# K and V in eight-partition groups: each group takes 1 MB that lies in one go in HBM

## The chip, the cores and the metric

The kernel runs on one core of a Trainium2 chip. The metric is the device time of one launch in microseconds, the median of several runs. A core has engines that work side by side and meet only through semaphores: PE (TensorE, matrix multiply, with its weight loads shown as PEld), DVE (VectorE), ACT (ScalarE), POOL (GpSimd) and SP (SyncE, which here only issues DMAs). Sixteen DMA engines move data between HBM, the large memory, and SBUF, the working memory of 128 partitions. One DMA that is issued on SP is shared out among them.

## The reference

One token is decoded. With g = sigmoid(sum of x times gate_w), the result is g times an attention block plus (1 - g) times a gated feed-forward block. The attention has 32 heads of 128, each over 65536 cached keys and values:

```python
q = (x @ wq).reshape(B, Sq, H, Dh).transpose(0, 2, 1, 3)        # one query per head
scores = jnp.einsum("bhqd,bhkd->bhqk", q, k_cache) * (Dh ** -0.5)
p = softmax(scores, axis=-1)
o = jnp.einsum("bhqk,bhkd->bhqd", p, v_cache)
a = o.transpose(0, 2, 1, 3).reshape(B, Sq, H * Dh) @ wo
b = (silu(x @ w_gate) * (x @ w_up)) @ w_down
return g * a + (1 - g) * b
```

All inputs are bf16. k_cache and v_cache have the shape [1, 32, 65536, 128]; a head of either is 16.78 MB. x has 512 elements, and the weights together are 14.0 MB.

## The kernel before

K and V pass through SBUF once. A head's 65536 rows are seen as 128 partitions times R = 512 rows. They are loaded in two halves, z = 0 and z = 1, of HR = 256 rows per partition each, so one load is 8.39 MB, with 64 KB for each partition. The view that a load reads is `kv_dram` (L200). In it the halves are the slowest dimension, then the partitions, then a partition's 256 rows: half z is one stretch of 8.39 MB in HBM, and partition p has the p-th 64 KB of it.

All loads go to one tile, `mem`, 184 KB per partition, in places that share it in turn: K half 0 at KA, K half 1 at KZ, V half 0 at VA and V half 1 at VZ. They overlap, so a load waits until the engines have read what it overwrites.

SP's program (L212 to L250) sets the order of the loads. The weights come first (L203 to L205). The first half of K of head 0 is issued as two loads of half the size (L219 to L222), with 32 KB for each partition, so that the work can begin on the first. Then come, for each head h from 1 on (L224 to L236): K half 0 of head h, V half 0 of head h - 1, K half 1 of head h, V half 1 of head h - 1. Before each stands a wait for DVE (`ktdone`) or PE (`pvdone`), which tells that the place is free. At the end come wo and the V of the last head, in eight pieces of falling size (`tail`, L59, issued at L239 to L245).

For K, DVE transposes blocks of 32 rows (L403 for half 0, L410 for half 1, L334 for head 0) into `kt`, and PE multiplies them with the head's query into the scores psS (L460): each partition and row gives one score, in one column of psS. ACT takes the exponential (L305), DVE shuffles its result into pb (L343), and PE multiplies pb with V into psO (L507), row by row of the places VA and VZ. For the last head, `piece` (L521) does the same with the pieces of the tail. A score of column r in partition p is multiplied by the row of V that lies in the same partition p and at the same row r; neither the largest score nor the sums ask which key that was.

## Time and profile before

| What | Value |
|---|---|
| Median of 3 runs | 2519.66 us (2519.46 to 2519.95) |
| The profiled execution's own time | 2521.24 us |
| Its span, from the first to the last instruction | 2519.9 us |
| Granted TensorE clock, mean | 0.71 |
| Busy: PE, PEld, DVE, ACT, POOL | 63%, 35%, 55%, 3%, 1% |
| Read from HBM | 1087.77 MB |

The page cuts the span into 40 slices of 63 us. For each it gives the busy share of the engines in tenths, the busy share of the core's 16 DMA engines, and the GB/s that they moved. Busy times of different engines lie beside each other and can't be added. A line of waits names who waited, for whom, the total in microseconds, how often, and the longest. A line of DMA issues gives a load's source, how many there were and the median time from issue to landing; it includes the time behind other loads in the queue.

### The profile page before, as it was taken

What the parts mean: (1) busy time and instruction counts of PE and PEld (TensorE: products, weight loads), DVE (VectorE), ACT (ScalarE), POOL (GpSimd) and SP (SyncE); (2) the same over time, 40 slices, a digit from 0 to 9 for tenths busy, and PEclk for the clock granted to TensorE, in tenths of its full rate; (3) what the DMA queues carried; (4) which work ended last, traced back from release to release, by engine and by line L of the source; (5) the groups of instructions that cost most, each with busy time, mean ns of one, the idle gap of its engine ahead of it and who ended that gap; (6) DMA issues with size and microseconds to landing.
All of it is one profiled execution on the core that took longest, in us unless ns stands there. A gap on an engine that the chain in (4) does not pass through costs nothing.

```text
span 2519.9 us, 46367 instructions
## 1 busy us (share of the span) xinstructions
PE 1586.7 (63%) x21432; PEld 890.3 (35%) x21432; DVE 1398.3 (55%) x1631; ACT 65.6 (3%) x195; POOL 26.8 (1%) x83
## 2 busy tenths in 40 slices
PE   3556756666666576565675665766656656567667
PEld 3333333333333333333333333333333333333334
DVE  3764565554654645646446555466464564654653
ACT  0000000000000000000000000000000000000000
POOL 0000000000000000000000000000000000000000
PEclk8567767677676676676776767767767667677676
DMA  9999999999999999999999999999999999999999
GB/s 420 434 433 433 433 434 433 433 433 433 434 434 433 433 432 435 433 434 435 433 433 436 434 435 433 433 434 433 433 435 433 434 432 433 433 433 434 432 433 387
DMA packets 20476, 1088.00 MB, mean 432 GB/s; under 512 B 2282, under 2 KB 2668, under 8 KB 2924
## 3 DMA queue, kind: packets, MB, share of 16 engines
q1 hardware_dynamic: 20452, 1087.78, 99.9%
q8 instruction: 11, 0.18, 0.0%
q14 instruction: 5, 0.04, 0.0%
q10 hardware_dynamic: 8, 0.00, 0.0%
HBM read 1087.77 MB, written 0.00 MB: 432 GB/s over the span
## 4 chain that ended last, share of the span: by engine, by line
DMA 73%; DVE 14%; issue 11%; PE 1%; DVEq 0%; SPq 0%; ACT 0%
DMA mem<-in_A_k_cache_dram 71%; DVE kt L410 7%; DVE kt L403 6%; DMA mem<-in_A_wo_dram 1%; PE psO L507 1%; DMA mem<-in_A_v_cache_dram 1%; DVE kt L334 0%; DVE pb L343 0%; DVEq L408 0%; SPq L205 0%; DVEq L401 0%; PE psS L460 0%; PE psZ L560 0%; SPq L220 0%; ACT fin L312 0%
## 5 line engine op out<-in xcount | busy, mean ns | idle before, releaser
L460 PE MATMUL psS<-qcur,kt 128*128 128x4 bf16 x16384 | 516.7, 167 | 886.1 <-DVE kt L403 552.0
L507 PE MATMUL psO<-mem,pb 128*4 128x512 bf16 x3968 | 1001.1, 418 | 17.4 <-DMA mem<-in_A_v_cache_dram 17.4
L403 DVE STREAM_TRANSPOSE kt<-mem 128x2048 uint32<-128x2048 uint32 x248 | 551.2, 2280 | 578.9 <-DMA mem<-in_A_k_cache_dram 577.9
L460 PEld LDWEIGHTS psS<-qcur,kt 128*128 128x128 bf16 x16384 | 474.0, 104 | 954.9 <-DVE kt L403 585.2
L410 DVE STREAM_TRANSPOSE kt<-mem 128x2048 uint32<-128x2048 uint32 x248 | 547.5, 2274 | 407.7 <-DMA mem<-in_A_k_cache_dram 407.7
L507 PEld LDWEIGHTS psO<-mem,pb 128*4 128x4 bf16 x3968 | 355.3, 91 | 619.8 <-issue 188.5
L343 DVE COPY pb<-pa 32x64 bf16<-32x64 bf16 x1024 | 234.1, 229 | 25.5 <-PE psO L507 10.7
L334 DVE STREAM_TRANSPOSE kt<-mem 128x2048 uint32<-128x2048 uint32 x16 | 35.4, 2275 | 17.0 <-DMA mem<-in_A_k_cache_dram 17.0
L348 DVE TENSOR_REDUCE sm<-psS 128x1 f32<-128x512 f32 x32 | 22.1, 691 | 35.5 <-PE psS L460 35.5
L299 ACT ACTIVATE oTn<-psT,gcol 128x1 bf16<-128x1 f32 x31 | 8.2, 263 | 1111.8 <-PE psT L487 1111.8
L278 POOL PARTITION_ALL_REDUCE sm<-sm x32 | 11.2, 351 | 2392.0 <-DVE sm L348 2392.0
L487 PEld LDWEIGHTS psT<-unit,orow 4*128 4x128 f32 x256 | 30.8, 186 | 14.9 <-issue 13.5
L487 PE MATMUL psT<-unit,orow 4*128 4x1 f32 x256 | 33.5, 248 | 0.8 <-ACT orow L297 0.8
L297 ACT ACTIVATE orow<-psO,sm 4x512 f32<-4x512 f32 x31 | 21.0, 677 | 447.7 <-issue 447.7
L303 ACT ACTIVATE sm<-sm 128x1 f32<-128x1 f32 x32 | 6.5, 203 | 831.7 <-POOL sm L278 831.7
L305 ACT ACTIVATE pa<-psS,sm 128x512 bf16<-128x512 f32 x32 | 22.0, 687 | 1.0
L521 PE MATMUL psW<-pb,mem 128*128 128x1 bf16 x512 | 14.4, 165 | 6.9 <-DMA mem<-in_A_v_cache_dram 5.7
L521 PEld LDWEIGHTS psW<-pb,mem 128*128 128x128 bf16 x512 | 13.9, 102 | 8.1 <-issue 6.4
L280 POOL PARTITION_ALL_REDUCE sm<-sm x32 | 12.3, 383 | 36.4 <-ACT pa L305 36.4
L444 PE MATMUL psM<-xTb,mem 128*128 128x1 bf16 x128 | 3.6, 166 | 11.6 <-DMA mem<-in_A_wq_dram 11.6
L536 PE MATMUL psY<-mem,oR 128*1 128x512 bf16 x31 | 9.6, 485 | 0.3 <-DVE oR L424 0.3
L430 DVE TENSOR_SCALAR w<-psW,sm 128x2 bf16<-128x2 f32 x1 | 0.2, 224 | 16.9 <-PE psW L521 16.9
(64 smaller groups left out, 62.0 us busy)
## 6 DMA issues: line engine op xcount, KB each, us to landing
mem<-in_A_v_cache_dram SPq DMA_DIRECT2D x3, 4096.0 KB, 28.9
mem<-in_A_k_cache_dram SPq DMA_DIRECT2D x2, 4096.0 KB, 38.7
mem<-in_A_wq_dram SPq DMA_DIRECT2D x1, 4096.0 KB, 13.1
mem<-in_A_wo_dram SPq DMA_DIRECT2D x1, 3968.0 KB, 34.3
mem<-in_A_v_cache_dram SPq DMA_DIRECT2D x1, 2048.0 KB, 33.4
mem<-in_B_w_gate_dram SPq DMA_DIRECT2D x1, 1792.0 KB, 16.9
mem<-in_B_w_up_dram SPq DMA_DIRECT2D x1, 1792.0 KB, 21.2
mem<-in_B_w_down_dram SPq DMA_DIRECT2D x1, 1792.0 KB, 25.0
```

The lines of the kernel that those rows point to most:

```text
L280: nc.gpsimd.partition_all_reduce(Lt, rsum, P, RADD).then_inc(s_L, 1)
L297: nc.scalar.mul(orow[0:4, :], psO[0:4, :], Li[0:4, :]).then_inc(s_or, 1)
L305: nc.scalar.activation(pa[:], psS[:], ACT.Exp, bias=nbias, scale=SCALE, accum_out=rsum).then_inc(expdone, 1)
L334: nc.vector.transpose(kt[:, i % 2, :].rearrange("p (j r t) -> p r j t", j=2, t=32), src.rearrange("p (r j t) -> p r j t", j=2, t=32)).then ...
L343: last = nc.vector.tensor_copy(dst, sr)
L348: nc.vector.reduce_max(mxs, psS[:], AX_X).then_inc(s_mx, 1)
L403: nc.vector.transpose(kt[:, c % 2, :].rearrange("p (j r t) -> p r j t", j=2, t=32), src.rearrange("p (r j t) -> p r j t", j=2, t=32)).then ...
L410: nc.vector.transpose(kt[:, c % 2, :].rearrange("p (j r t) -> p r j t", j=2, t=32), src.rearrange("p (r j t) -> p r j t", j=2, t=32)).then ...
L460: last = nc.tensor.matmul(psS[:, col + 4 * r:col + 4 * r + 4], ktb[c % 2][:, je // 2, r, :, je % 2], qcur[:, je, :], start=(je == 0), stop ...
L487: last = nc.tensor.matmul(psT[:, 0:1], orow[0:4, i * Dh:(i + 1) * Dh], unit[0:4, i:i + 1], start=(i == 0), stop=(i == 3))
L507: last = nc.tensor.matmul(psO[0:4, :], pb[:, 256 * z + r:256 * z + r + 4], vt[:, r * Dh:(r + 4) * Dh], start=(z == 0 and part == 0 and m = ...
L521: last = nc.tensor.matmul(psW[:, 0:1], vt[:, r * Dh:(r + 1) * Dh], pb[:, col:col + 1], start=(col == 0), stop=(col == R - 1))
```

## The change

The view of a head's rows in HBM changes. Before, the dimensions were, slowest first, half (b, 2), partition (p, 128), row (r, 256). After, they are group (e, 16), half (b, 2), partition within the group (k, 8), row (r, 256). Partition p is now 8e + k. Eight partitions together hold one stretch of 1 MB, of which half 0 is the first 512 KB and half 1 the second. One load is then 16 stretches of 512 KB, one every 1 MB. The destination is the same [128, n] slice of `mem` as before. The view has one dimension more, so the column slices of the first K load and of the tail get one more colon. The tail uses the same view. `lanes` is a new function around the destination that returns its argument.

```diff
         def kv_dram(cache, h):
-            return cache[0, h].rearrange("(b p r) d -> b p (r d)", b=2, p=P)
+            return cache[0, h].rearrange("(e b k r) d -> b e k (r d)", b=2, k=8, e=16)
+
+        def lanes(ap):
+            return ap
...
-                sp.dma_start(at(place(kind, h, z), HR * Dh), kv_dram(cache, h)[z]).then_inc(d[kind + "az"[z]], 16)
+                sp.dma_start(lanes(at(place(kind, h, z), HR * Dh)), kv_dram(cache, h)[z]).then_inc(d[kind + "az"[z]], 16)
...
-                sp.dma_start(at(KA + 32 * n, half), kv_dram(A_k_cache, 0)[0][:, n * half:n * half + half]).then_inc(
+                sp.dma_start(lanes(at(KA + 32 * n, half)),
+                             kv_dram(A_k_cache, 0)[0][:, :, n * half:n * half + half]).then_inc(
                     (d["ka0"], d["ka"])[n], 16)
...
-            src = A_v_cache[0, H - 1].rearrange("(b p r) d -> b p (r d)", b=2, p=P)
+            src = kv_dram(A_v_cache, H - 1)
...
-                sp.dma_start(at(kb, nr * Dh), src[b][:, o * Dh:(o + nr) * Dh]).then_inc(dt_[n], 16)
+                sp.dma_start(lanes(at(kb, nr * Dh)), src[b][:, :, o * Dh:(o + nr) * Dh]).then_inc(dt_[n], 16)
```

## The prediction

> **What bounds the kernel now.** I read the page first, its parts 1 to 3, to see which resource is full; then the stretches of the span, to see whether it is full in every stage; then the DMA queue's issues and waits, to see whether it ever runs dry; then the chain.

> ```profile
> span 2519.9 us, 46367 instructions
> PE 1586.7 (63%) x21432; PEld 890.3 (35%) x21432; DVE 1398.3 (55%) x1631; ACT 65.6 (3%) x195; POOL 26.8 (1%) x83
> DMA  9999999999999999999999999999999999999999
> GB/s 420 434 433 433 433 434 433 433 433 433 434 434 433 433 432 435 433 434 435 433 433 436 434 435 433 433 434 433 433 435 433 434 432 433 433 433 434 432 433 387
> DMA packets 20476, 1088.00 MB, mean 432 GB/s; under 512 B 2282, under 2 KB 2668, under 8 KB 2924
> q1 hardware_dynamic: 20452, 1087.78, 99.9%
> ```

> No engine that computes is over 63% busy. SP's queue keeps the 16 DMA engines busy for 99.9% of the span, and the rate is the same line of 432 to 436 GB/s in every slice but the first and the last. That is 433 / 16 = 27.1 GB/s for each DMA engine. A rate so level, whatever else is going on, is that of a fixed path, not of a memory that is busier at one time than at another.

> ```profile
> 200.00:600.00 400.00, 253.77 (x3379) 140.81 (x3376) 228.32 (x256) 10.07 (x30) 3.67 (x10) 0.70 1.00 434
> 1000.00:1077.40 77.40, 49.91 (x653) 27.47 (x652) 43.46 (x50) 2.02 (x6) 0.73 (x2) 0.71 1.00 434
> 2000.00:2400.00 400.00, 258.58 (x3311) 140.95 (x3312) 218.20 (x252) 11.14 (x34) 4.40 (x12) 0.71 1.00 434
> ```

> The columns are window, length, busy time of PE, PEld, DVE, ACT and POOL, granted TensorE clock, DMA share and GB/s. The second row is one head: in 77.4 us the DMA never rests, PE works 49.9 us and DVE 43.5 us.

> ```profile
> mem<-in_A_k_cache_dram SPq DMA_DIRECT2D x63, 29.7
> mem<-in_A_v_cache_dram SPq DMA_DIRECT2D x62, 26.1
> SPq L216 <- PE psO L507: 1314.4, 61, 25.0
> DVE kt L403 <- DMA mem<-in_A_k_cache_dram: 577.9, 30, 19.6
> DVE kt L410 <- DMA mem<-in_A_k_cache_dram: 407.7, 31, 13.7
> DMA 73%; DVE 14%; issue 11%; PE 1%; DVEq 0%; SPq 0%; ACT 0%
> ```

> A load of half a head is 32768 x 128 x 2 B = 8.39 MB, 19.4 us at 433 GB/s. From issue to landing a K load takes 29.7 us and a V load 26.1 us, so a load waits 10.3 or 6.7 us behind the one before it: the queue has no gaps, although SP waits for free buffers. DVE waits for K 985.6 us in all. The chain's 11% "issue" and 14% DVE are steps of that same wait for K, beside DMA that goes on working.

> **The sum that the change acts on.** K and V are 32 x 2 x 16.78 MB = 1073.7 MB of the 1087.8 MB, 98.7%. Of the 99.9% x 2519.9 = 2517.4 us of DMA, 2484.9 us are K and V. The profiled execution took 2521.2 us, 1.3 us more than its span and 1.6 us over the median of 2519.66; the sum is made against 2521.2, and 1.6 is taken off at the end.

> **The change part by part.**

> *The issue on SP.* The source gets one more dimension (16 groups of 8 runs in place of 128 runs). L216 shows an issue at 328 ns; there are 125 of those, and 2 + 8 others for K and V. The trace has no issue with such a source; the others on SP take 400 to 530 ns (the weights' issues, L205). I bound it between 0 and +0.33 us each, 0 to 41 us on SP for the 125. The cover is the 6.7 us that each load is issued ahead of its turn, so I take 0; without the cover it would be those 41 us. Behind an issue in SP's program stands the next wait for a buffer, which lasts up to 25.0 us, and nobody waits for SP itself.

> *The runs.* A partition's share of a load is 256 rows, 64 KB in one piece in HBM, before and after; the first K load's two halves have 32 KB each. The 128 runs of a load, and the 20476 packets, should stay. Cost 0, the cover being none: if runs were cut smaller it would be seen in the packet count.

> *Which rows lie where.* Column r of partition p now holds another key; K and V change alike, and a softmax with its weighted sum doesn't depend on the order of keys. No instruction of PE, DVE, ACT or POOL is added or moved, no wait is added. `lanes` returns what it is given. The tail's eight pieces take the same columns from the new view.

> *Where the 16 engines read.* Before, a load is one stretch of 8.39 MB, neighbouring partitions 64 KB apart. After, it is 16 stretches of 512 KB, one every 1 MB. Unknown; bounded under rival 2 and rival 3 from both sides.

> *Which engine writes which partitions.* This decides. The trace does not tell which DMA engine serves which partition. Before, both sides of the copy count 128 rows outermost. After, the source counts 16 outermost and the destination 128. If the work is dealt out by the outermost dimension, engine e can only get source group e, and with it the eight neighbouring partitions 8e to 8e+7. The present deal, whatever it is, lets 16 engines write at 27.1 GB/s each without ever meeting. A new deal need not have that property. If two engines have to write through one path, each gets half while they meet. Let f be the share of a load during which they meet: the price is f x 2484.9 us, between 0 (they never meet: rival 1) and 2484.9 (always). A load of 8 runs then takes 8 x 64 KB / 27.1 GB/s = 19.4 us x (1 + f).

> I take f near its upper end, 0.95. The row nearest to it is the DMA line: all 16 engines are at work at once from start to end, with a level rate, so they go through their eight runs nearly in step, and two that meet at a run's start meet to its end. An engine pair that gets ahead runs out of issued loads (there is about one in the queue) and starts the next beside its partner, in step again; and a load only counts as landed when its slowest pair is done. So 0.95 x 2484.9 = 2360.7 us, and 2521.2 + 2360.7 - 1.6 = 4880 us.

> [...]

> *What is late next.* With a head's load at about 151 us (77.4 x 1.95), DVE (43.5 us) and PE (49.9 us) wait longer for K and V, buffers come free long before their turn, and SP's queue stays full. Nothing else comes onto the path.

> **The rivals.**

> *1. No change (time 2519.7, within 2515 to 2524.6, that is 0.2%, about what a measurement of this kernel can tell from none).* Engines keep their partitions, or they have no path in common, and an engine is at its 27.1 GB/s anyhow. For it: the rate is level in all stages, so a DMA engine's own speed is a natural limit, and the number and size of runs stay. Against it: the source's outermost count changes from 128 to 16, which is the only thing that such a deal can go by.

> *2. HBM gives less (2597).* Sixteen streams at whole multiples of 1 MB, in step, may press on the same part of HBM. For it: before, the streams are spread over one stretch. Against it: they are at multiples of 64 KB already, and the rate doesn't suffer. Price from the slowest slices: 420 GB/s (the first, with the start in it) would give 2484.9 x (433/420 - 1) = +77 us, 387 (the last, with small pieces in it) +295 us; I take 420 as the one with long runs. [...]

> *3. Faster (2503).* One engine now reads 512 KB in one go, in place of runs that it has to find anew; if HBM rows opened anew cost it something, the rate could rise to the best slice, 436 GB/s: 2484.9 x (1 - 433/436) = 17 us less. It decides from 433.9 GB/s on (5 us less). Against it: over 400 us the rate is 434 in both long windows, so the 436 is the scatter of a slice.

> [...]

> **How the numbers follow.** Forecast 0.40; rival 1 0.26; rival 2 0.12; rival 3 0.06; rival 4 0.16. The likeliest is the forecast, 4880 us, with a range of its own of 4500 (f = 0.8) to 5010 (f = 1). The range for 8 in 10 has to reach down to the case of no change, whose weight of 0.26 can't be left out: 2516 to 5010. Slower by over 0.2%: 0.40 + 0.12 + 0.16 = 0.68; within 0.2%: 0.26; faster: 0.06.

> **What the profile of the changed kernel would show.** Forecast: the GB/s line at about 222 (433 / 1.95) in all slices of K and V, with the DMA line still at 9 and some 20476 packets; DVE's wait for K in L403 and L410 at some 3300 us; the first slices, where the weights load, at the old rate. Rival 1: the same lines as before. Rival 2: the GB/s line a few per cent lower with DMA at 9. Rival 3: 434 or more. [...] If the packet count changes, my reading of the runs was wrong; if the queue's share falls under 99%, SP's issues have come onto the path. The prediction is wrong if the work isn't dealt by the outermost dimension, or if the engines have no path in common.

## The result: 2.06 times the time

The changed kernel takes 5179.4 us (median of 6 executions, 5141.1 to 5210.2) where the kernel before takes 2519.66 us: 2.056 times as long, with a 95% interval of 2.047 to 2.065. The forecast was 4880 us, with a range up to 5010. The direction came out as forecast, and the runs below fit the mechanism; the size came out 6% too small, and the range ended too low.

The profiled execution took 5171.7 us. These are parts 1 to 3 of its page:

```profile
span 5170.4 us, 46367 instructions
DMA  9999999999999999999999999999999999999999
GB/s 246 210 206 210 209 209 207 209 209 207 210 210 210 210 210 209 209 209 211 209 211 210 210 209 208 211 209 211 210 210 208 210 210 210 210 210 209 209 209 211
DMA packets 20476, 1088.00 MB, mean 210 GB/s; under 512 B 2282, under 2 KB 2668, under 8 KB 2924
q1 hardware_dynamic: 20452, 1087.78, 100.0%
```

The same 20476 packets move the same bytes, and the 16 DMA engines are busy all the time, as before. Only the rate has fallen, from 433 to 210 GB/s, level over the whole span. So a packet takes about twice as long (64 KB take 5.01 us in the mean, where they took 2.42), and nothing else shows on the DMA side: no gaps, no smaller pieces.

The stretches of time, with the columns as in the prediction, show what this does to the engines:

```profile
200.00:600.00 400.00, 122.06 (x1614) 67.88 (x1613) 105.25 (x109) 5.10 (x16) 2.21 (x6) 0.60 1.00 209
3000.00:3400.00 400.00, 120.81 (x1616) 67.44 (x1615) 112.00 (x141) 4.71 (x13) 1.47 (x4) 0.61 1.00 210
```

In 400 us PE is busy for 121 to 122 us (before: 254 to 259) and DVE for 105 to 112 us (before: 218 to 228). They do the same work at half the pace. The waits, the loads' time to landing and the issues on SP say the same:

```profile
DVE kt L407 <- DMA mem<-in_A_k_cache_dram: 1841.8, 31, 61.2
DVE kt L414 <- DMA mem<-in_A_k_cache_dram: 1691.9, 31, 54.9
SPq L219 <- PE psO L511: 2466.4, 61, 42.5
mem<-in_A_k_cache_dram SPq DMA_DIRECT2D x63, 70.9
mem<-in_A_v_cache_dram SPq DMA_DIRECT2D x62, 69.1
L219 SPq DMA_DIRECT2D mem<-in_A_k_cache_dram x63: 536/537/542, 17.3 to 4968.8; - x63
```

DVE waits 3533.7 us for K, where it waited 985.6 us. A load now takes 8.39 MB / 210 GB/s = 40 us, and lands 69 to 71 us after its issue, so it is issued some 30 us ahead of its turn. One issue takes 537 ns of SP's time, where it took 328 ns; those 125 x 0.21 = 26 us are hidden by the 30 us of lead.

### The packets, one by one

Behind the DMA line lie the start and the duration of every packet. The record names no engine, but each packet begins where another ends, and so they can be chained into 16 sequences of 1000 packets of 64 KB. Durations in ns, from the middle of one such sequence of either kernel:

```
before  2422 2426 2419 2422 2422 2418 2422 2422 ...   mean of all 16000: 2422
after   4906 5099 5099 5036 4891 5100 5102 5027 4899 5101 5101 5025 4895 5099 5102 5028 ...   mean of all 16000: 5012
```

After the change the durations repeat every four packets: in this sequence two of 5.10 us, one of 5.03 and one of 4.90. That would fit two engines that write through one path for four packets, go on to the next path for four more, and are a little out of step: around the change of path there would be a short time in which one is alone and goes at its full speed. This is my reading; no trace shows a path, or which two engines share one. The 16 sequences stay together from start to end: their packets of the same number begin within 4.2 to 5.4 us of each other, about the length of one packet (before: 1.5 to 2.4 us).

### The profile page after: what moved, and what is told of

It is laid out like the page before. It is cut to its first block, busy times and chain, and to the rows that moved or that the text cites. A ratio compares the mean times of both kernels' runs of the same rounds, so it can differ in the third digit from the quotient of the medians.

```text
span 5170.4 us, 46367 instructions
## 1 busy us (share of the span) xinstructions
PE 1594.0 (31%) x21432; PEld 894.3 (17%) x21432; DVE 1398.0 (27%) x1631; ACT 65.6 (1%) x195; POOL 27.0 (1%) x83
## 2 busy tenths in 40 slices
DMA  9999999999999999999999999999999999999999
DMA packets 20476, 1088.00 MB, mean 210 GB/s; under 512 B 2282, under 2 KB 2668, under 8 KB 2924
## 3 DMA queue, kind: packets, MB, share of 16 engines
q1 hardware_dynamic: 20452, 1087.78, 100.0%
## 4 chain that ended last, share of the span: by engine, by line
another core or an unknown queue 70%; DVE 19%; issue 9%; PE 1%; DMA 1%; DVEq 0%; SPq 0%; ACT 0%
DVE kt L407 8%; DVE kt L414 6%; DVE pb L347 4%; DMA mem<-in_A_k_cache_dram 1%; DVE kt L338 1%; PE psS L464 1%; PE psW L525 0%; PE psY L540 0%; DVE sm L359 0%; DVEq L395 0%; DVEq L412 0%; SPq L208 0%; DVE sm L352 0%; DVEq L405 0%
## 5 line engine op out<-in xcount | busy, mean ns | idle before, releaser
L491 PEld LDWEIGHTS psT<-unit,orow 4*128 4x128 f32 x256 | 30.8, 186 | 14.9 <-issue 13.5
```

The source lines that it names most:

```text
L491: last = nc.tensor.matmul(psT[:, 0:1], orow[0:4, i * Dh:(i + 1) * Dh], unit[0:4, i:i + 1], start=(i == 0), stop=(i == 3))
```

## The experiments

The theory under test, called "deal": the 16 groups outermost give each engine eight neighbouring partitions, and two engines then always write through one path into SBUF. A "path" is the theory's word for what two engines would have to share; no trace names one, and which partitions belong to one is inferred from rates and packet times alone. The main rival, "HBM": 16 streams at multiples of 1 MB press on one part of HBM. Where a time is given "beside" that of the kernel before, each of the two is a single execution.

### The deal without the addresses

```diff
-            return cache[0, h].rearrange("(e b k r) d -> b e k (r d)", b=2, k=8, e=16)
+            return cache[0, h].rearrange("(b k e r) d -> b e k (r d)", b=2, k=8, e=16)
```

> The source still counts 16 groups outermost, each eight partitions, but neighbouring groups now lie 64 KB apart in HBM and the eight runs of a group 1 MB apart, so that at any step the 16 engines read one stretch of 1 MB. Theory 'deal' (each engine gets eight neighbouring partitions, and two engines always write through one path into SBUF): as slow as the changed kernel, 5130 to 5220 us, if the 5% over twice the time belong to the sharing; 4950 to 5010 us if they belong to the 1 MB spacing. Theory 'HBM' (16 streams 1 MB apart press on one part of HBM): the spacing in step is gone, so 2515 to 2530 us.

Measured: 5172.9 us, 2.055 times the kernel before (2.051 to 2.058). The GB/s line of its page:

```profile
GB/s 246 211 208 208 208 210 207 209 208 210 210 207 210 209 210 209 209 209 210 209 210 210 207 210 208 211 209 210 208 209 209 211 210 209 209 209 210 210 210 215
```

The same rate with other addresses, and a step's reads lie side by side. The runs in the middle of four take 5.10 us here too. So the loss, and also what goes beyond twice the time, has nothing to do with the 1 MB between the groups.

### The addresses without the deal

```diff
-            return cache[0, h].rearrange("(b p r) d -> b p (r d)", b=2, p=P)
+            pair = cache[0, h // 2 * 2:h // 2 * 2 + 2].rearrange("x s d -> (x s) d")
+            quarter = pair.rearrange("(p q r) d -> q p (r d)", q=4, p=P)
+            return quarter[h % 2 * 2:h % 2 * 2 + 2]
```

The tail reads through the same view.

> The source counts 128 partitions as before, but a partition's 64 KB lie 256 KB apart, across two heads, so that four neighbouring partitions are 1 MB; the heads of a pair are mixed, so what is computed is no longer the reference's attention, while bytes, loads and instructions stay. Theory 'deal': the same as before, 2515 to 2530 us. Theory 'HBM': streams at multiples of 1 MB, so slow, 4900 us or more.

Measured: 2519.58 us, a ratio of 1.000 (0.9991 to 1.0009). The GB/s line:

```profile
GB/s 422 431 433 434 433 434 433 434 433 433 433 433 433 433 433 433 433 433 433 434 433 433 433 434 433 434 433 433 434 433 433 433 433 433 433 433 434 436 433 395
```

Streams 256 KB apart, and 1 MB between sets of four, cost nothing. With these two runs the rival "HBM" has fallen.

### 128 KB for each partition in HBM, with the count of 128 kept

```diff
-            return cache[0, h].rearrange("(b p r) d -> b p (r d)", b=2, p=P)
+            return cache[0, h].rearrange("(p b r) d -> b p (r d)", b=2, p=P)
```

The tail's view is changed in the same way.

> A partition holds 128 KB that lie in one go, of which the first load takes the first half; the source counts 128 partitions, 128 KB apart. The result is the reference's. Theory 'deal': 2515 to 2525 us, the change of addresses without the change of the deal. Theory 'HBM': some loss from power-of-two spacing, over 2600 us. If longer pieces in HBM gained anything it would show here as under 2514 us.

Measured: 2519.69 us, a ratio of 1.000 (0.9991 to 1.0009). Neither a loss nor a gain. A load still reads only 64 KB of each partition's 128 KB, so what it reads in one go has not become longer: before, the neighbours' 64 KB joined on; here they lie 128 KB apart. The run shows that pieces of 64 KB that don't join cost nothing.

### Fewer partitions under a DMA

Four kernels have the addresses of the kernel before, but cut each load into several DMAs by partitions. The semaphores' targets rise with the number of DMAs. Shown is the first; the others differ in the slices.

```diff
-                sp.dma_start(at(place(kind, h, z), HR * Dh), kv_dram(cache, h)[z]).then_inc(d[kind + "az"[z]], 16)
+                for s in (slice(0, 64), slice(64, 128)):
+                    sp.dma_start(at(place(kind, h, z), HR * Dh)[s], kv_dram(cache, h)[z][s]).then_inc(
+                        d[kind + "az"[z]], 16)
```

> The addresses of the kernel before, but each load of 128 partitions (all but the first two and the tail) is cut into two, one for partitions 0 to 63 and one for 64 to 127; same runs of 64 KB, 123 loads more. Theory 'deal' with paths that serve partitions 32 apart: with 64 partitions there are only half of the paths under each load, two engines on each, so again 5000 to 5250 us. Theory 'HBM': reading 4 MB at a time in one stretch can't hurt, 2520 to 2560 us. If paths were shared only because of the 16 groups of eight, 2520 to 2560 us too.

Measured: 5126.2 us, the median of two executions, 2.035 times the kernel before (2.030 to 2.039). No group of eight is left here, source and destination both count 64, the addresses are the old ones, and still:

```profile
GB/s 280 208 210 210 212 208 211 210 210 210 209 210 210 210 209 209 210 209 210 209 210 209 209 211 208 211 209 210 209 210 208 210 208 210 208 209 209 209 209 270
```

A rate of 210 GB/s is a little under half of 433, about what half of the paths would give, so 64 neighbouring partitions seem to reach only half of them. If a path were four neighbouring partitions alone, 64 partitions would have 16 of them and no engines would have to meet.

`slice(0, 128, 2), slice(1, 128, 2)`:

> As halves, but the two DMAs of a load take the even and the odd partitions, 64 each, so that both sides count 64 and every path is under each DMA. Theory 'only 128 against 128 is dealt so that engines don't meet': engine e has partitions 8e, 8e+2, 8e+4, 8e+6 and meets engine e+4: 5000 to 5250 us, with a period of two runs in place of four. Rival: equal counts are enough for the good deal: 2520 to 2560 us.

Measured: 2519.5 us beside 2520.1 of the kernel before. My expectation failed and its rival held: 64 against 64 keeps the full rate of 433 GB/s when the partitions span all 128.

`[slice(32 * g, 32 * g + 32) for g in range(4)]`:

> As halves, but four DMAs of 32 neighbouring partitions each per load, two partitions per engine. Within one DMA no two partitions are 32 apart, so only neighbours can share. Theory 'four neighbouring partitions are one path': engines 2j and 2j+1 meet, with two engines on each of 8 paths: 5.1 us a run, 5050 to 5250 us, less if engines get a whole DMA apart. Rival 'only partitions 32 apart share': 2520 to 2560 us.

Measured: 5147.8 us beside 2519.8. Within 32 partitions none are 32 apart, and still the rate is 206 to 210 GB/s in all slices but the first and the last. So partitions closer than that share, too; the time lies in the range for two engines on each of 8 paths, which fits four neighbours to a path but doesn't show the paths.

`[slice(g, 128, 4) for g in range(4)]`:

> As quarters, but each of the four DMAs takes every fourth partition (32 of them, over all 128), so every path is under each DMA with two partitions. Theory 'a deal of 32 or more that spans all 128 partitions gives each engine partitions of one path': 2515 to 2560 us. Rival 'a deal is in plain order below 64': engine e has partitions 8e and 8e+4, meets engine e+4 on both, 5000 to 5250 us.

Measured: 2522.4 us beside 2519.8. Cutting a load in four costs next to nothing here, 2.6 us, when every part spans all 128 partitions. These are the GB/s lines of the even and odd partitions, then of the quarters:

```profile
GB/s 420 429 435 435 434 434 434 433 433 433 433 433 433 433 433 433 433 433 433 433 434 433 433 433 433 433 433 433 433 434 433 434 433 433 433 433 433 435 434 397
```

```profile
GB/s 280 206 208 207 208 207 209 206 209 206 209 207 209 207 209 206 210 206 210 207 208 207 209 207 208 207 209 207 209 207 209 207 209 207 209 208 208 208 208 279
```

The bytes, the runs of 64 KB and the addresses in a load are the same in both. What differs is which partitions are written at one time, and with them which addresses are read at one time. The addresses alone have been seen to do nothing, in the two experiments above.

### Sixteen partitions under a DMA

`[slice(16 * g, 16 * g + 16) for g in range(8)]`:

> As halves, but eight DMAs of 16 partitions each per load: one partition per engine, four engines on a path, 4 paths at a time. Without a loss in sharing a run takes 4 x 2.42 = 9.69 us, in all 9900 to 10000 us. If each path loses the 5% that two engines lose (5.11 in place of 4.84 us), 10.2 us and 10350 to 10550 us. If the loss grows with the number of engines on a path, over 10700 us.

Measured: 8080.8 us beside 2520.1, and none of the three expectations fits. Nine in ten packets take 7.80 to 8.24 us, with a mean of 7.97, 3.3 times 2.42. If a path carries no more than one engine's 27.1 GB/s, four engines on one path for the whole time would take at least 9.69 us. That 16 neighbours have four paths is an assumption of mine that no run shows. If it holds, the engines of a path would have to be apart for some of the time: an engine that is one DMA ahead writes the next 16 partitions, which by the theory would have other paths. The chained sequences agree with this in part: an engine has one packet of each DMA, and at nearly every moment the 16 are spread over two DMAs or three. Which engines then share a path the record doesn't tell, so the 7.97 us are not worked out.

### Other numbers of groups

```diff
-            return cache[0, h].rearrange("(e b k r) d -> b e k (r d)", b=2, k=8, e=16)
+            return cache[0, h].rearrange("(e b k r) d -> b e k (r d)", b=2, k=16, e=8)
```

> The source counts 8 groups outermost, each 16 partitions with 2 MB in one go. Theory 'deal by the outermost count, paths shared by partitions 32 apart': only 8 engines can work, engine e has partitions 16e to 16e+15, engines e and e+2 write through one path, so only 4 paths work at a time with two engines on each. A load is 16 runs of 5.1 us = 81.6 us, 128 such loads, 10300 to 10550 us in all, about 105 GB/s. Rival: 8 engines, but nothing shared: 8 x 27.1 = 217 GB/s, 4950 to 5050 us. Rival: the deal looks at the destination's 128 partitions only: about 5180 us as with 16 groups.

Measured: 9820.5 us beside 2520.1. Its DMA lines:

```profile
DMA  5455445545454554544554454544445455554554
GB/s 139 112 116 117 115 103 106 108 107 107 108 106 106 108 109 111 114 110 106 105 106 106 107 105 105 107 107 108 118 105 110 115 115 109 111 111 112 113 113 137
q1 hardware_dynamic: 19372, 1087.77, 50.1%
```

Eight of 16 engines work (the packets of 64 KB chain into eight sequences, and the busy share is half), and each again at half its speed: 108 / 8 = 13.5 GB/s, where one had 27.1. The theory's two halvings are there. The time lies 5% under its range. Two thirds of the packets take 4.8 to 5.1 us, but one in seven takes 2.8 to 4.5 us, which fits engines that are less well in step.

`k=2, e=64`:

> The source counts 64 groups outermost, each two partitions with 256 KB in one go. Theory 'the deal follows both sides' counts unless both are 128': each engine gets four groups, that is again the eight neighbouring partitions 8e to 8e+7, so 5130 to 5220 us. Rival: any count that is a multiple of 16 and closer to the 128 partitions is dealt as before: 2515 to 2530 us.

Measured: 2520.5 us beside 2520.1. The expectation failed: with counts of 64 and 128 the time is that of 128 and 128.

`k=4, e=32`:

> The source counts 32 groups outermost, each four partitions with 512 KB in one go. 16 groups were slow and 64 were not. Theory 'a group can't be split between engines, and an engine's good share is two sets of four partitions 32 apart': groups of four can be dealt in that way, so 2515 to 2530 us. Rival 'the good deal needs at least 64 outermost' : each engine gets two neighbouring groups, that is 8e to 8e+7, and 5130 to 5220 us.

Measured: 2521.3 us beside 2519.8.

```profile
span 2519.9 us, 46367 instructions
GB/s 419 434 433 434 431 434 433 433 433 433 434 433 433 433 434 433 431 434 433 433 433 434 433 433 433 433 433 434 437 433 432 431 433 435 436 433 434 434 434 392
```

So it isn't the count of 128 that matters, nor that both sides count alike. Groups of two and of four partitions are harmless (2520.5 and 2521.3 us), groups of eight are not (5179.4). This fits the theory's share of an engine, two sets of four neighbours: groups of up to four could be put together to such shares, and a group of eight could not be split. No trace shows the shares. A rule by the count alone, that the outermost count must be at least 32, would fit these kernels as well, and no run here separates the two. 32 groups keep 512 KB in one go for each four partitions (256 KB of it in one load), at the full rate.

### V alone

```diff
+            if cache is A_k_cache:
+                return cache[0, h].rearrange("(b p r) d -> b p (r d)", b=2, p=P)
             return cache[0, h].rearrange("(e b k r) d -> b e k (r d)", b=2, k=8, e=16)
```

The first K load's slices are those of the kernel before.

> Only V is laid out in groups of eight partitions, K as before; scores and V then belong to different keys, so what is computed is no longer the reference's attention, while bytes and loads stay. The change added 5171.7 - 2521.2 = 2650.5 us over 128 loads of half a head, 20.7 us each. Theory 'each load dealt in that way pays for itself, the engines of a pair start it in step': half of the loads, 2521 + 1325 = 3846 us, 3800 to 3880 us. Rival 'the good loads between let the pairs get out of step': under 3700 us.

Measured: 4058.3, 4095.5, 4123.0 and 4548.2 us in four executions, where the kernel before takes 2519.6; the two shortest are 1.618 times as long (1.611 to 1.626). The profiled execution is the shortest, and it is already 212 us over the sum, the opposite of the rival. Eight packets of a V load and the eight of a K load behind it, from one sequence, in ns:

```
V  4919 5119 5120 5115 4932 5119 5081 5118   K  3438 4382 3087 2475 2426 2418 2419 2420
```

The V load is as slow as when all loads are so. The first three packets of the K load aren't at 2.42 us. I read this as engines that reach the K load at different times, so that those in it write to paths on which others still finish their V load; no run tests that. It is only half of the extra time. The 1000 packets of an engine take 3808 us in the mean, where 63 K loads and 62 V loads at their own pace would take 3707: 101 us more. For another 2.8% of the span, some 113 us, the DMA engines stand idle, where before it was 0.1%: by the packets' times only two engines are at work during 98 us, against 1 us in the kernel before and in the changed one. I read this as two that lag and hold up a load, while the other fourteen run out of issued loads. A change of deal from load to load costs extra here, at least 212 us; the price isn't just that of the slow half. The rate swings with it:

```profile
GB/s 384 275 255 281 244 268 256 251 266 241 268 239 279 238 271 267 253 272 240 279 254 273 279 248 280 277 255 286 268 272 288 268 273 295 271 269 290 279 265 214
q1 hardware_dynamic: 20452, 1087.78, 97.2%
```

## Why the prediction was right, and where it was wrong

**What bounds the kernel** was right in that it is the DMA. The addresses don't set its rate: kernels with other addresses keep the mean of 432 GB/s, and only those lose it in which partitions are dealt in another way. That the level 433 GB/s is that of a fixed path, as I wrote, no run shows by itself.

**The issue on SP.** I bounded the dearer issue by 0 to +0.33 us and took 0 for its effect. It costs +0.21 us and is hidden, as said. The longest wait for a buffer behind an issue of L216 is 37.6 us, not 25.0, which I took from the largest group of waits alone; nothing hangs on it.

**The runs, and which rows lie where.** The packet count is the same, and no engine does other work, as said.

**How long two engines meet.** I took f = 0.95, an estimate that no trace of the kernel before shows. The packets give (5012 - 2422) / (5105 - 2422) = 0.965, where 5105 ns is what the packets in the middle of four take. That they keep in step all along was right for this kernel. One of my reasons for it was not: I let an engine that gets ahead run out of issued loads, but with a DMA share of 100.0% and loads issued 30 us ahead none does. What holds them together the runs don't show, so there is some luck in how near 0.95 came. Rival 4 of the chances stands for engines that meet, but out of step, for half of the time (f = 0.5, 3762 us). No run shows that 0.5; the packets of this kernel give 0.965. What fits engines that are partly out of step is seen with 8 groups, where one packet in seven takes 2.8 to 4.5 us, and with 16 partitions to a DMA, where the engines are spread over two DMAs or three.

**The price of meeting: the step that failed.** I wrote that two engines on one path "each gets half while they meet", and so took 2484.9 us as the price of meeting always. A packet beside another takes 5.105 us, not 2 x 2.422 = 4.844 us. Two engines that meet get 2 x 65536 B / 5.105 us = 25.7 GB/s together, where one alone gets 27.1. The price of always meeting is thus (5105 / 2422 - 1) x 2484.9 = 2753 us, not 2484.9. With f = 0.965 the sum is 2521.2 + 2657 = 5178 us; the profiled execution took 5171.7. As f and the price both come from its packets, this shows only that nothing beside the packets' length has changed. The signs that I named in the profile are off in the same direction: 210 GB/s in place of 222, and a wait of DVE for K of 3533.7 us in place of some 3300. The upper end of my range, 5010, was the end of a bound that left no room for a loss in the sharing itself. It should have been open upwards.

The 5% isn't a matter of HBM: packets in the middle of four take the same 5.10 us with the addresses of the changed kernel and with those of the first experiment, and 5.11 to 5.12 us in the halves and quarters, which read one stretch. What loses it, the runs don't show.

**Which partitions share a path.** The runs show only rates and times: halves (64 neighbours) take 2.035 times as long, quarters (32 neighbours) 5147.8 us, even and odd partitions 2519.5 us, every fourth 2522.4 us. The expectations assume more than that, namely which partitions a path serves: these four runs fit it, and none shows a path.

**Rival 2, HBM,** is out: 1.000 (0.9991 to 1.0009) with the streams spread at multiples of 256 KB and 1 MB. A pitch of over 256 KB between neighbouring partitions was tried only in the first experiment, with 1 MB, where the engines already meet: its packets are no longer than those of the changed kernel.

**Rival 3, faster through longer pieces,** is out as far as the runs reach: pieces that don't join (64 KB at a pitch of 128 or 256 KB) take 2519.69 and 2519.58 us, no longer than the joined ones of before, and of two kernels whose engines meet, 512 KB in one go in the one (the changed kernel) and 64 KB in the other (the first experiment) take the same 5.10 us a packet.

None of the layouts beats the kernel before. At 433 GB/s with all 16 engines busy, the order of bytes in HBM had nothing to give in those tried here.

## What to carry to other kernels

When a kernel is bound by DMA, an access pattern that keeps bytes, runs and packet count can still halve the rate, here from 433 to 210 GB/s; as I read it, by a deal that makes engines meet. Try what kept the rate here: on the HBM side groups of at most four neighbouring partitions (2520.5 and 2521.3 us with two and four, 5179.4 and 9820.5 with eight and sixteen), and DMAs that each span all 128 partitions (2519.5 and 2522.4 us, where 64 and 32 neighbours took 5126.2 and 5147.8). The sign of it in the profile here is a DMA share of 100% with a lower, level GB/s line and an unchanged packet count of 20476. When a price is bounded by "two share one", leave the upper end open: here a shared packet took 5.105 us, not 4.844.

## What the runs showed that I had not expected

- Two engines that meet, as I read the packets of 5.105 us, get 25.7 GB/s together, one alone 27.1.
- A DMA of 64 or of 32 partitions loses at most 0.1% if they span all 128 (2519.5 and 2522.4 us) and half the rate if they are neighbours (2.035 times, 5147.8 us).
- The kernel before repeats within 0.02% (2519.46 to 2519.95 us; in all its executions beside the first experiments 2519.2 to 2520.7), the changed one within 1.3% (5141 to 5210 us), and V alone only within 12% (4058 to 4548 us). How far two engines of a pair are out of step may differ from one execution to the next; that is my reading, and no run tests it.
- The two deals in turn, load by load (V alone), cost at least 212 us more than half of the change's price: longer packets, and engines that stand idle at times.
